# A gated linear attention and a maxout FFN in one kernel: the 64x64 products of two units put into one run

## The chip, the cores and the metric

One core of one Trainium2 chip runs the whole program. The metric is the device time of one execution in microseconds, as the median of the runs shown. The engines are named as in the profile: PE (TensorE matmul, with its weight loads as PEld), DVE (VectorE), ACT (ScalarE), POOL (GpSimd) and SP, whose queue issues nearly all of the DMAs.

## The reference

The first half is a linear attention with a gate for each feature, for 4 batches, 8 heads, 768 tokens and 48 features; its output goes, token by token, into an FFN whose hidden layer is the largest of three products. All is float32.

```python
f = 1.0 / (1.0 + np.exp(-f_logit))
for t in range(S):
    state = f[:, :, t, :, None] * state + np.einsum('bhd,bhe->bhde', k[:, :, t], v[:, :, t])
    y[:, :, t] = np.einsum('bhd,bhde->bhe', q[:, :, t], state)
x = attn_out.transpose(0, 2, 1, 3).reshape(B * S, H * D)          # 3072 x 384
h = np.maximum(np.maximum(x @ w1, x @ w2), x @ w3)                # 384 -> 768
out = h @ w_out                                                   # 768 -> 384
```

## The kernel before

**Units.** The attention is cut into 24 units. A unit is a chunk of 64 tokens (`C`) of two batches (`a` = 0, 1) with all 8 heads (four pairs `hp`, each with an even and an odd head, `par` = 0, 1). Unit u works on chunk u // 2 and on batches 2(u % 2) and 2(u % 2) + 1, so unit u continues the states that unit u - 2 left. Four units make a group of 512 tokens (`GRP`, `TOK`), and each group has one FFN.

**The products of a unit on PE.** They are 64x64 products, four to a set (one for each `par` and `a`), which run beside each other in the four quarters of the array:

- `pairs` (L400): keys times queries of the chunk, into the two-bank tile `a`; DVE then multiplies them by the causal mask into `at` (L403);
- `sums` (L437): keys times values, the chunk's contribution to the state, into the other half of the same banks; DVE adds it to the decayed state (`new_state`, L452), and POOL decays the result for the unit after next (`carry`, L361);
- `values` (L419): `at` times values, into the two-bank tile `y`; ACT then reads one element of `y` into `seen` (L426);
- the products of the queries with the state, in `finish` (L508), added to the same `y`; then ACT copies `y` into the FFN's input `xT` (L515), and `pack` moves rows of it by DMA.

Before that, DVE turns the loaded blocks (L300), runs two scans (L333, L351), and turns the scaled keys back, 16 transposes a unit in four parts (`keys_by_blocks`, L386); POOL makes the scaled keys `kh` (L344) and queries `qh` (L355).

**The FFN on PE.** Full 128x128 products: `inputs_by_pairs` (L884) and `outputs_by_pairs` (L633), for groups 1 to 5; group 0 has its own form with L546 and L787. Both use four PSUM banks, two called `p` and two called `tr`. In the inputs, three pairs of hidden blocks n = 0, 1, 2 go through seven steps; the steps of n use one `tr` bank `B[n]` and one `p` bank `A[n]`. `third(n)` ends with DVE reading `B[n]` (L927), `fourth(n)` with DVE reading `A[n]` (L934) and taking the maximum with the rest (L935). In the outputs, `a` is a `p` bank and `b` and `c` are the two `tr` banks; `add(o_of(0, 0), b, 0)` has DVE read `b` (L641).

**What sets the order.** The order is written by hand: inside `tc.manual_schedule()` each engine has its instructions in the order of the code, and semaphores are added where one reads or overwrites what another has written. The FFN is a generator that yields the cost of what it just issued; `fill(ns)` lets it go on until the costs come to ns. The main loop over units calls `fill` five times a unit, and the attention's steps lie between these calls. In unit u the 64x64 products come in one piece: `values(u - 1)`, `sums(u - 1)`, `pairs(u)`, `finish(u - 1)`. After the last unit, `values(23)` and `finish(23)` come as two more pieces. The name "run of unit u" below means that piece.

**PSUM.** Eight banks: `p` 2, `tr` 2, `a` 2, `y` 2. The pools hand out `p` and `tr` banks in turn.

## Time and profile before

| what | value |
|---|---|
| runs | 405.4, 407.33, 407.48 us; median 407.33 us |
| profiled execution, span from first to last instruction | 403.7 us |
| median of the runs less that span | 3.6 us |
| PE busy | 390.9 us (97%) |
| DVE busy | 297.7 us (74%) |
| POOL busy | 256.4 us (64%) |
| ACT busy | 180.9 us (45%) |
| mean granted TensorE clock | 0.999 |

The execution that was profiled has a span of 403.7 us; its own time with what lies around the span is not given apart, so a change in the span is added to the median of the runs. In rows of the timeline the columns are start in us from the span's start, duration in us, engine, line, operation, out<-in, and the number of instructions merged into the row; a float32 product is two instructions, so that the 16 products of a step stand as x32. A duration reaches to the modelled end of the last matmul, which lies past the start of what follows.

### The profile page before, as it was taken

What the parts mean: (1) busy time and instruction counts of PE and PEld (TensorE: products, weight loads), DVE (VectorE), ACT (ScalarE), POOL (GpSimd) and SP (SyncE); (2) the same over time, 40 slices, a digit from 0 to 9 for tenths busy, and PEclk for the clock granted to TensorE, in tenths of its full rate; (3) what the DMA queues carried; (4) which work ended last, traced back from release to release, by engine and by line L of the source; (5) the groups of instructions that cost most, each with busy time, mean ns of one, the idle gap of its engine ahead of it and who ended that gap; (6) DMA issues with size and microseconds to landing.
All of it is one profiled execution on the core that took longest, in us unless ns stands there. A gap on an engine that the chain in (4) does not pass through costs nothing.

```text
span 403.7 us, 11683 instructions
## 1 busy us (share of the span) xinstructions
PE 390.9 (97%) x4658; PEld 339.7 (84%) x4658; DVE 297.7 (74%) x572; ACT 180.9 (45%) x431; POOL 256.4 (64%) x283
## 2 busy tenths in 40 slices
PE   5988999999999999999999999999999999999995
PEld 4766765559998889998889988899988889988995
DVE  6997897999989999897998997998995450002600
ACT  3478787422224442345532344523354425586120
POOL 2189695879997697296587277667477850435700
PEclk9999999999999999999999999999999999999999
DMA  8999986767574576576635477634573003541002
GB/s 171 233 282 284 279 214 89 153 92 150 82 96 114 69 154 135 104 120 84 131 104 97 62 113 88 156 78 81 75 157 91 1 19 87 143 136 70 2 19 63
DMA packets 181611, 47.21 MB, mean 117 GB/s; under 512 B 160497, under 2 KB 179249, under 8 KB 181553
## 3 DMA queue, kind: packets, MB, share of 16 engines
q1 hardware_dynamic: 177536, 45.52, 54.7%
q10 hardware_dynamic: 4016, 0.91, 1.1%
q8 instruction: 37, 0.61, 0.6%
q14 instruction: 22, 0.17, 0.1%
HBM read 37.75 MB, written 4.72 MB: 105 GB/s over the span
## 4 chain that ended last, share of the span: by engine, by line
PE 90%; SPq 4%; DMA 1%; ACT 1%; issue 1%; POOL 1%; DVE 0%
PE p L884 20%; PE p L633 18%; PE tr L884 16%; PE tr L633 14%; PE p L546 7%; PE y L419 3%; PE p L787 3%; PE a L400 2%; PE y L508 2%; PE a L437 2%; SPq L178 2%; DMA v_ld<-in_v_dram 1%; SPq L164 1%; SPq L222 1%; PE tr L295 1%
## 5 line engine op out<-in xcount | busy, mean ns | idle before, releaser
L386 DVE STREAM_TRANSPOSE ks<-kh 32x128 f32<-32x128 f32 x256 | 77.5, 303 | 11.5 <-POOL kh L344 7.4
L884 PE MATMUL tr<-xT,placed 128*128 128x256 f32 x180 | 44.4, 384 | 0.0
L343 POOL COPY ends<-r 128x8 f32<-128x8 f32 x24 | 8.6, 358 | 48.1 <-DVE r L333 48.1
L884 PEld LDWEIGHTS tr<-xT,placed 128*128 128x128 f32 x180 | 33.5, 190 | 4.9
L344 POOL TENSOR_TENSOR kh<-kt,r 128x512 f32<-128x512 f32 x18 | 31.9, 1772 | 8.5 <-DVE kt L300 8.5
L333 DVE TENSOR_TENSOR_SCAN r<-gate,from_one 128x520 f32<-128x520 f32 x24 | 33.2, 1382 | 5.4 <-ACT gate L312 2.8
L546 PE MATMUL p<-xT,w_in 128*128 128x256 f32 (+1 forms) x108 | 33.9, 458 | 3.0 <-POOL w_in L756 1.9
L597 POOL TENSOR_TENSOR w_in<-hm 128x256 f32<-128x256 f32 x18 | 13.3, 737 | 32.2 <-DVE hm L935 29.4
L515 ACT COPY xT<-y 64x256 f32<-64x256 f32 (+1 forms) x60 | 22.1, 368 | 22.4 <-PE y L508 21.7
L351 DVE TENSOR_TENSOR_SCAN prod<-gate,from_inv 128x520 f32<-128x520 f32 x24 | 31.6, 1317 | 0.0
L884 PE MATMUL tr<-xT,w_in 128*128 128x256 f32 x120 | 30.8, 379 | 0.0
L641 DVE TENSOR_TENSOR o<-tr,w_in 128x384 f32<-128x384 f32 (+1 forms) x11 | 5.7, 521 | 33.4 <-PE tr L633 29.0
L884 PE MATMUL p<-w_in,placed 128*128 128x256 f32 x120 | 30.4, 382 | 0.0
L633 PE MATMUL p<-placed,hm 128*128 128x192 f32 x144 | 29.7, 333 | 0.0
L546 PEld LDWEIGHTS p<-xT,w_in 128*128 128x128 f32 x108 | 19.5, 190 | 12.0 <-issue 6.0
L884 PE MATMUL p<-xT,placed 128*128 128x256 f32 x120 | 29.2, 379 | 0.0
L633 PE MATMUL tr<-w_out,w_in 128*128 128x192 f32 x144 | 28.6, 326 | 0.0
L927 DVE TENSOR_TENSOR hm<-tr,hm 128x512 f32<-128x512 f32 x15 | 10.3, 684 | 22.8 <-PE tr L884 15.9
L262 POOL TENSOR_TENSOR w_in<-top_bits,rest_bits 128x384 uint32<-128x384 uint32 x18 | 21.7, 1216 | 7.2 <-DVE top_bits L256 4.3
L884 PEld LDWEIGHTS p<-w_in,placed 128*128 128x128 f32 x120 | 22.4, 190 | 4.4 <-issue 1.5
L638 ACT COPY w_in<-p 128x384 f32<-128x384 f32 x15 | 7.2, 479 | 41.0 <-PE p L633 41.0
L284 ACT ACTIVATE raw<-top_bits 128x384 f32<-128x384 f32 x48 | 25.2, 526 | 0.4
(168 smaller groups left out, 995.6 us busy)
## 6 DMA issues: line engine op xcount, KB each, us to landing
raw<-in_moe_w_dram SPq DMA_DIRECT2D x24, 384.0 KB, 4.4
v_ld<-in_v_dram SPq DMA_DIRECT2D x48, 96.0 KB, 3.4
placed<-in_moe_w_dram SPq DMA_DIRECT2D x12, 384.0 KB, 6.3
out_dram<-o SPq DMA_DIRECT2D x45, 96.0 KB, 2.2
placed<-in_moe_w_out_dram SPq DMA_DIRECT2D x6, 384.0 KB, 5.4
f_ld<-in_f_logit_dram SPq DMA_DIRECT2D x36, 64.0 KB, 2.7
k_ld<-in_k_dram SPq DMA_DIRECT2D x36, 64.0 KB, 2.5
q_ld<-in_q_dram SPq DMA_DIRECT2D x36, 64.0 KB, 2.6
```

What stands on the lines that cost most here:

```text
L262: nc.gpsimd.tensor_tensor(dst, by(top), by(rest), op=ALU.add)
L284: nc.scalar.activation(over, size, AF.Relu, scale=(-1 / HI_MIN, 1.0)[step - 1], bias=(1.0, -HI_END * (1 - 2.0 ** -24))[step - 1], accum_ou ...
L333: nc.vector.tensor_tensor_scan(r[:, 0:LEN][:, ::-1], flat(gate)[:, ::-1], flat(from_one)[:, ::-1], 1.0, op0=ALU.mult, op1=ALU.max)
L344: (nc.vector if u < BY_ROWS else nc.gpsimd).tensor_tensor(kh.rearrange("p h a t -> p a h t"), kt, by_batch(r[:, 1:LEN + 1].rearrange("p (x ...
L351: nc.vector.tensor_tensor_scan(flat(prod), flat(gate_tiles[u % 2]), flat(from_inv[u % 2]), 1.0, op0=ALU.mult, op1=ALU.max)
L386: nc.vector.transpose(ks[n * 32:(n + 1) * 32, :, par, e0:e0 + 32], kh[p0:p0 + 32, :, a, t0:t0 + 32])
L419: nc.tensor.matmul(y[o:o + DP, a, hp * C:(hp + 1) * C], lhsT=v_ld[s, 2 * hp + par, :], rhs=d["at"][s, par, hp, :], start=(hp == 0), stop=F ...
L515: nc.scalar.copy(xT[o, :, t0 + a * C:t0 + (a + 1) * C], y[i, a, 0:HP * C].rearrange("p (h t) -> p h t", h=HP))
L546: nc.tensor.matmul(p if w < TOK else p.rearrange("p (two t) -> p two t", two=2), lhsT=w_in[i][:, kt, j * 128:(j + 1) * 128], rhs=x[:, t.st ...
L597: engine.tensor_tensor(dst, x, y, op=op)
L633: nc.tensor.matmul(b[:, p * HD:(p + 1) * HD], lhsT=x, rhs=w, start=id(b) not in begun, stop=True, skip_group_check=True)
L884: nc.tensor.matmul(b[:, j * HALF:(j + 1) * HALF], lhsT=w[:, (2 * n + j) * 128:(2 * n + j + 1) * 128], rhs=x, start=begin and j == 0, stop= ...
```

## The change

From unit 9 on, a run has the 64x64 products of two units. Units 9, 11, ..., 23 have no such products of their own. The runs of units 10, 12, ..., 22 and a last one, called unit 24, hold in this order: `pairs(u - 1)`; `sums` of u - 2 and half of u - 1 (`sums_apart`); `values(u - 2)`; `values(u - 1)`; the other half of the sums; DVE's two additions `new_states`; `pairs(u)`; the state products of u - 2 and of u - 1 (`with_state`); then the copies `to_x` of both and one `pack`. The run of unit 24 has neither sums nor `pairs(u)`.

The two units share the tiles: `y` and the pairs take the left or the right half of each of their banks. The sums go to one `p` and one `tr` bank of the FFN, those that it would use next; `fill_to_free` lets the FFN go on to a place where these hold nothing that is still needed (after a `fourth`, or after `add(o_of(0, 0), b, 0)` in the outputs). The `p` and `tr` banks become fixed tiles in turn, and the states of both units one tile each. The parts of `keys_by_blocks` move to other places between the calls of `fill`, of which there are still five a unit.

```diff
+            def psum(nm, ahead=False):
+
+                t = rooms[nm][turn_of[nm] % 2]
+                turn_of[nm] += not ahead
+                return t
...
+            all_states = keep.tile([128, 2, 2, HP * D], FP32, name="st")
+            states = [all_states[:, :, bp] for bp in range(2)]
+            all_carried = keep.tile([128, 2, 2, HP * D], FP32, name="state")
...
 def pairs(u, p=None):
+                at0 = u % 2 * HP * C if u > FIRST else 0
...
-                        nc.tensor.matmul(p[t, par, hp * C:(hp + 1) * C], lhsT=kh[r, hp, a, :], rhs=qh[r, a, hp, :],
+                        nc.tensor.matmul(p[t, par, at0 + hp * C:at0 + (hp + 1) * C], lhsT=kh[r, hp, a, :], rhs=qh[r, a, hp, :],
...
-            def values(u):
+            def values(u, y=None, first=True):
...
+                if u >= FIRST:
+                    y = y[:, :, u % 2 * HP * C:(u % 2 + 1) * HP * C]
...
+            def sums_apart(u, lanes, hps=range(HP)):
+
+                d, v_ld = ready[u], v_tiles[u % NLD]
+                Y = u % 2 * HP * D
+                for hp in hps:
+                    for par, a in FOUR:
+                        s = slice(a * C, (a + 1) * C)
+                        nc.tensor.matmul(lanes[a][par * DP:(par + 1) * DP, Y + hp * D:Y + (hp + 1) * D],
+                                         lhsT=d["ks"][s, 2 * hp + par, :], rhs=v_ld[s, 2 * hp + par, 0:D],
+                                         start=True, stop=True)
+
+            def new_states(lanes):
+                for a in range(2):
+                    flat_of = lambda t: t[:, a].rearrange("p b x -> p (b x)")
+                    nc.vector.tensor_tensor(flat_of(all_states), lanes[a][:, 0:2 * HP * D], flat_of(all_carried), op=ALU.add)
...
+            def fill_to_free():
+                while not free[0]:
+                    advance()
...
-                for u in range(GRP, NU):
+                for u in range(GRP, NU + 1):
...
+                    run = u <= FIRST or u % 2 == 0
...
+                    elif run:
+                        fill_to_free()
+                        room_of_unit, y = room_of_pairs(), room_of_y()
+                        lanes = [psum(nm, ahead=True) for nm in ("p", "tr")]
+                        pairs(u - 1, room_of_unit)
+                        if u < NU:
+                            sums_apart(u - 2, lanes)
+                            sums_apart(u - 1, lanes, range(HP // 2))
+                        values(u - 2, y)
+                        values(u - 1, y, False)
+                        if u < NU:
+                            sums_apart(u - 1, lanes, range(HP // 2, HP))
+                            new_states(lanes)
+                            pairs(u, room_of_unit)
+                        for i in (2, 1):
+                            with_state(u - i)
+                        for i in (2, 1):
+                            to_x(u - i, xT)
...
+                    if u > FIRST:
+                        keys_by_blocks(u, 0)
+                        if not run:
+                            keys_by_blocks(u, 1)
+                        fill(part)
...
+                    elif run:
+                        carry(u)
+                        carry(n)
+                        keys_by_blocks(u, 1)
+                        keys_by_blocks(u, 2)
                     else:
-                        values(u)
+                        keys_by_blocks(u, 2)
+                        keys_by_blocks(u, 3)
...
-                    if n == NU:
-                        finish(u, xT)
-                        pack(3, 3, xT, both)
-                        packed[u // GRP] = xT
-                    keys_by_blocks(n, 0)
-                    fill(part - 1000 if u < 2 * GRP else part)
-                    keys_by_blocks(n, 1)
+                    if u < FIRST:
+                        keys_by_blocks(n, 0)
+                        fill(part - 1000)
+                        keys_by_blocks(n, 1)
+                    elif u == FIRST:
+                        fill(part)
+                    elif run:
+                        keys_by_blocks(u, 3)
```

**What it does to the order.** The lines of the changed kernel are later by some: `pairs` is L416, `sums_apart` L529, `values` L441, the state products L551, the FFN's inputs L930 and outputs L676; on DVE `at` is L419, `new_states` L536, the readers of the FFN's banks L973, L980, L981 and L684, the transposes of the keys L401. The words in square brackets name the semaphores that an instruction waits for, by the engine that raises them.

PE at the run of unit 14, before (`fourth(0)` of the inputs ends, then values and sums of unit 13, pairs of 14, state products of 13, and the inputs go on):

```order
L884 MATMUL p_2364<-w_in1_64,placed1_135 128x256
L419 MATMUL y_2574<-at_2427,v_ld1_127 64x64 [waits DMAHW4_49,DVE_49,PE_49]
L419 MATMUL y_2574<-at_2427,v_ld1_127 64x64
L419 MATMUL y_2574<-at_2427,v_ld1_127 64x64 [waits DMAHW5_49]
L419 MATMUL y_2574<-at_2427,v_ld1_127 64x64 x13
L437 MATMUL a_2573<-v_ld1_127,ks_2337 64x48 [waits DVE_49]
L437 MATMUL a_2573<-v_ld1_127,ks_2337 64x48
L437 MATMUL a_2573<-v_ld1_127,ks_2337 64x48 [waits DVE_49] x2
L437 MATMUL a_2573<-v_ld1_127,ks_2337 64x48 x12
L400 MATMUL a_2573<-qh_2509,kh_2502 64x64 [waits Pool_49]
L400 MATMUL a_2573<-qh_2509,kh_2502 64x64 x15
L508 MATMUL y_2574<-qh_2296,state_2313 48x64 [waits Activation_49]
```

The same engine and place after the change, the start of the run: the last product of `fourth(0)` into bank `p1_89`, the pairs of unit 13, and the first sums of unit 12, which go to that same `p1_89` and to `tr0_86`:

```order
L930 MATMUL p1_89<-w_in1_64,placed1_139 128x256
L416 MATMUL a_2397<-qh_2207,kh_2200 64x64 [waits PE_49]
L416 MATMUL a_2397<-qh_2207,kh_2200 64x64 x15
L529 MATMUL p1_89<-v_ld0_130,ks_2176 64x48 [waits DMAHW1_49,DVE_49]
L529 MATMUL p1_89<-v_ld0_130,ks_2176 64x48
L529 MATMUL tr0_86<-v_ld0_130,ks_2176 64x48 [waits DMAHW2_49]
```

And the middle of that run: values of unit 12, values of unit 13 in the other half of the same tile `y_2398`, and the rest of the sums. The value that the Activation semaphore has to reach there is the one that the copy `seen` of unit 12 raises, the DVE value is that of `at` of unit 13, and the DVE value in the fence above is that of L980, which reads `p1_89`:

```order
L441 MATMUL y_2398<-at_2132,v_ld0_130 64x64 [waits PE_49]
L441 MATMUL y_2398<-at_2132,v_ld0_130 64x64 x15
L441 MATMUL y_2398<-at_2415,v_ld1_131 64x64 [waits DVE_49,Activation_49]
L441 MATMUL y_2398<-at_2415,v_ld1_131 64x64 x15
L529 MATMUL p1_89<-v_ld1_131,ks_2303 64x48 x2
```

What moved: the run has 256 products instead of 128 and starts with pairs; its values wait for a mask product and for a copy of the same run, and its sums for the reader of an FFN bank.

DVE before and at the run of unit 16, before (turning and scanning for unit 16, sums of the FFN's input, keys, the reader of the outputs' bank `b`, keys, then `at` of unit 16):

```order
L300 STREAM_TRANSPOSE kt<-k_ld_116 128x512
L351 SCALAR_TENSOR_TENSOR prod<-gate_99,from_inv_95 128x520
L300 STREAM_TRANSPOSE qt<-q_ld_118 128x512
L597 TENSOR_TENSOR xT_146<-xT_146 128x2x128
L597 TENSOR_TENSOR s_last<-xT_146 128x256
L386 STREAM_TRANSPOSE ks<-kh 32x4x32 x4
L641 TENSOR_TENSOR o<-tr,w_in_63 128x2x192
L386 STREAM_TRANSPOSE ks<-kh 32x4x32 x8
L403 TENSOR_TENSOR at<-a,mask 128x512
L452 TENSOR_TENSOR st_142<-a,state 128x384
```

The same place after the change (`at` of unit 15, the two state sums and `at` of unit 16 belong to the run):

```order
L310 STREAM_TRANSPOSE kt<-k_ld_120 128x512
L364 SCALAR_TENSOR_TENSOR prod<-gate_103,from_inv_99 128x520
L310 STREAM_TRANSPOSE qt<-q_ld_122 128x512
L640 TENSOR_TENSOR xT_150<-xT_150 128x2x128
L640 TENSOR_TENSOR s_last<-xT_150 128x256
L401 STREAM_TRANSPOSE ks<-kh 32x4x32 x8
L684 TENSOR_TENSOR o<-tr_87,w_in_63 128x2x192
L419 TENSOR_TENSOR at<-a,mask 128x512
L536 TENSOR_TENSOR st<-p_89,state 128x384
L536 TENSOR_TENSOR st<-tr_87,state 128x384
```

What moved: eight transposes of the keys (of unit 15, whose `kh` is a unit old) stand ahead of the reader of `b` instead of four of unit 16; and the bank `tr_87` that this reader frees is the one that the run's sums are written to.

## The prediction

> **What bounds the kernel now.** I read the page first: busy shares, slices and the chain.

> ```profile
> span 403.7 us, 11683 instructions
> PE 390.9 (97%) x4658; PEld 339.7 (84%) x4658; DVE 297.7 (74%) x572; ACT 180.9 (45%) x431; POOL 256.4 (64%) x283
> PE   5988999999999999999999999999999999999995
> DVE  6997897999989999897998997998995450002600
> PEclk9999999999999999999999999999999999999999
> PE 90%; SPq 4%; DMA 1%; ACT 1%; issue 1%; POOL 1%; DVE 0%
> ```

> PE is full from the fourth slice to the last, at full clock, and it is 90% of the chain that ended last. So a microsecond saved in PE's own sequence is a microsecond of the span, and so is each one in which PE is made to wait. DVE is second, at nine tenths for as long as there is attention (to slice 30). A window there says how near it is:

> ```profile
> 200.00:220.00 20.00, 20.00 (x227) 18.68 (x227) 18.54 (x36) 7.04 (x18) 15.34 (x16) 1.00 0.52 113
> ```

> DVE, the fourth figure, works 18.5 of 20 us. Whatever makes PE wait for DVE will find it late more often than idle.

> **What the change removes: nine changes between full and 64x64 products.** The timeline of PE around the run of unit 14:

> ```profile
> 188.34 1.03 PE L884 MATMUL p<-xT,w_in 128*128 128x256 f32 x4
> 189.20 1.03 PE L884 MATMUL p<-rest_bits,placed 128*128 128x256 f32 x4
> 190.07 1.03 PE L884 MATMUL p<-w_in,placed 128*128 128x256 f32 x4
> 191.02 0.69 PE L419 MATMUL y<-at,v_ld 64*64 64x64 f32 x32
> 191.54 0.63 PE L437 MATMUL a<-v_ld,ks 64*64 64x48 f32 x32
> 191.99 0.66 PE L400 MATMUL a<-qh,kh 48*64 48x64 f32 x32
> 192.47 0.63 PE L508 MATMUL y<-qh,state 48*48 48x64 f32 x32
> 193.03 1.99 PE L884 MATMUL tr<-xT,placed 128*128 128x256 f32 x8
> 194.86 0.38 PE L884 MATMUL p<-w_in,placed 128*128 128x256 f32 x1
> ```

> Four full products take 0.865 us from start to start (188.34, 189.20, 190.07), but the four ahead of the run take 0.95: 0.09 lost going in. The run lasts 2.01 us where four steps of 0.465 (between L437's 0.45 and L400's 0.48) would be 1.86: 0.16 at its two ends. The eight after it take 1.83 instead of 1.73: 0.10 more. Together 0.36 us a run, the same to 0.01 at the other whole runs.

> ```profile
> 117.77 0.69 PE L419 MATMUL y<-at,v_ld 64*64 64x64 f32 x32
> 329.26 0.69 PE L419 MATMUL y<-at,v_ld 64*64 64x64 f32 x32
> 332.68 0.67 PE L508 MATMUL y<-qh,state 48*48 48x64 f32 x32
> ```

> From unit 9 (the first row) on there are 15 runs before and the two pieces of unit 23 (the other rows), 17; after, eight: units 10, 12, ..., 24. The numbers of products and of FFN steps are the same. **Gain: 9 x 0.36 = 3.24 us.**

> **What it adds, first: the copy `seen` inside the run.** Before, it is raised and used 0.93 us apart, with sums and pairs between (191.54 to 192.47). After, PE goes from the values of u - 2 straight to those of u - 1, whose first product waits for the copy made after the last product of u - 2, as the order shows. That round trip is in the trace:

> ```profile
> 191.79 0.15 ACT L426 COPY seen<-y 1x1 f32<-1x1 f32 x1 [0.77 <-PE y L419]
> 66.78 0.14 ACT L426 COPY seen<-y 1x1 f32<-1x1 f32 x1
> 66.97 0.67 PE L508 MATMUL y<-qh,state 48*48 48x64 f32 x32
> ```

> In unit 14 ACT had been idle for it and the copy ended at 191.94; at 66.92 a copy ended late and PE's L508 started 0.05 after. So PE could go on at 191.99, where its next step began at 191.54: 0.45 us. L508 at 66.97 also took 0.67 rather than 0.63: 0.04 to get going again. **Loss: 0.45 in each of units 10 to 22, 7 x 0.45 = 3.15.** Bounds: 0.3 (the copy and one hand-over) to 0.8 (ACT busy with a 0.48 us copy).

> [...]

> **Second: sums in the bank that `fourth` has just filled.** In units 10, 14, 18 and 22 the free place is the end of a `fourth`, and the sums' `p` bank is the one that DVE's L934 must still read.

> ```profile
> 191.20 0.69 DVE L934 SCALAR_TENSOR_TENSOR hm<-hm,p 128x512 f32<-128x512 f32 x1 [1.48 <-PE p L884]
> 191.81 0.68 DVE L935 SCALAR_TENSOR_TENSOR hm<-hm,top_bits 128x512 f32<-128x512 f32 x1
> L403 DVE TENSOR_TENSOR at<-a,mask x24: 678/692/693, 12.1 to 324.4; 128x512 f32<-128x512 f32 x24
> ```

> This is that very `fourth(0)`, with DVE waiting for it: the read ends at 191.89, PE hears of it at 191.95. The run's pairs, 0.51 with the start, would let the sums begin at 191.53. **Loss: 4 x 0.42 = 1.68**, with 0 as the lower bound and 1.5 each where DVE is late. The mask product `at` of u - 1 then runs from 192.42 to 193.11 (0.69 behind L935), and the values that need it come at 191.95 + 0.70 of sums + 0.46 + 0.45 = 193.56: hidden, by 0.4 us. If DVE is later than that, PE waits for it too. DVE itself stands idle from there until the last sums, about 1.4 us a run.

> **Third: sums in the outputs' bank `b`.** In units 12, 16 and 20 the `tr` bank of the sums is `b`, which PE left 5 us ago but which DVE reads (L641, now L684) only when it gets there. Before, at unit 16:

> ```profile
> 206.67 0.69 DVE L927 TENSOR_TENSOR hm<-tr,hm 128x512 f32<-128x512 f32 x1
> 207.37 1.26 DVE L386 STREAM_TRANSPOSE ks<-kh 32x128 f32<-32x128 f32 x4
> 208.64 0.69 DVE L403 TENSOR_TENSOR at<-a,mask 128x512 f32<-128x512 f32 x1
> 209.81 1.26 DVE L386 STREAM_TRANSPOSE ks<-kh 32x128 f32<-32x128 f32 x4
> 220.37 1.24 DVE L386 STREAM_TRANSPOSE ks<-kh 32x128 f32<-32x128 f32 x4 [1.08 <-POOL kh L344]
> 221.65 0.56 DVE L641 TENSOR_TENSOR o<-tr,w_in 128x384 f32<-128x384 f32 x1
> 205.22 1.03 PE L884 MATMUL tr<-xT,placed 128*128 128x256 f32 x4
> 208.18 1.13 PE L884 MATMUL p<-rest_bits,placed 128*128 128x256 f32 x4
> 221.16 0.69 PE L419 MATMUL y<-at,v_ld 64*64 64x64 f32 x32
> ```

> DVE reads `b` from 221.65 to 222.21, after the run has begun. From `third(2)`'s reader at 206.67 to there are 15.54 us. After the change `at` and its state sum (208.64 to 209.81) are not in this stretch, the wait for `kh` goes, since the keys are of the unit before, and four transposes more (1.27) come in: 15.54 - 1.17 - 1.08 + 1.27 = 14.56. It cannot begin before `third(2)` ends, which after the change is right ahead of `fourth(2)` (208.18, call it F): the four products reach 0.17 past F, DVE starts 0.10 later (191.20 against 190.07 + 1.03). So `b` is free at F + 0.27 + 14.56 + 0.05 = F + 14.88. PE from F to the run takes 221.16 - 208.18 = 12.98, less 0.11 for no run ahead, and 0.51 of pairs: the sums want the bank at F + 13.38. **Loss: 3 x 1.5 = 4.50.** Bounds: 0, if DVE has less to do there, and 2.6, since a row of the same view shows what its operations can take beside POOL:

> ```profile
> 203.62 1.75 DVE L935 SCALAR_TENSOR_TENSOR hm<-hm,top_bits 128x512 f32<-128x512 f32 x1
> ```

> That is 1.06 above its 0.68. I take 1.5, as the rows of this very stretch give it; the 1.75 falls in a place where DVE would otherwise wait for `third(2)`.

> **Unit 24** has no sums to hide behind. `at` of 23 ends 0.74 + 0.69 + 0.06 = 1.49 us after the pairs begin, values of 22 are over at 0.97: 0.52 us; then the state products wait for the last `seen`: 0.45. **Loss 0.97.** Sixteen restarts in all (7 + 4 + 3 + 2) at 0.04: **0.64**.

> **What costs nothing.** Moved keys, scans and `carry` keep their number; the keys' `kh` and the decayed state are now made a unit ahead, and DVE no longer waits for POOL there. `pack` comes as often as before; after unit 24's run some 38 output products of 0.325 us, 12.4 us, hide copies of 2.3, the transfer and POOL's sums of `xT`. The state sums end, by DVE, at about the time that PE leaves the run; if later, the next `tr` step waits for the rest.

> **Sum.** -3.24 + 3.15 + 1.68 + 4.50 + 0.97 + 0.64 = +7.7 us on the span of 403.7. On the median of 407.33, which is 3.6 above the span, that is 415.0.

> **Rivals.**
> - *The run's waits are covered (faster).* Had PE work between, as at `seen` before, only the switches would count: 407.33 - 3.24 = 404.1. The point is 0.40 us of waiting a run, on average over the eight. For it: PE never waits for `seen` from unit 9 on now. Against: the round trip alone measures 0.45, with nothing put between.
> - *DVE reaches `b` in time*, the rest as forecast: 415.0 - 4.5 - 0.12 = 410.4. For it: DVE loses its waits for `kh` and reads `b` only 0.5 us after the run's start now. Against: the 14.56 against 13.1 us above.
> - *Neither bank makes PE wait*: 410.4 - 1.68 - 0.16 = 408.6, which one can hardly tell from no change.
> - *DVE becomes the bound.* With 18.5 of 20 us busy and 1.4 us more of standing still in each run, one slow operation (+1.06) in each half of a group is handed to PE: 415.0 + 7 x 1.06 = 422.4.

> **How the numbers follow.** Forecast 0.55, with a range of its own from 412 to 418; `b` in time 0.15; neither bank 0.10; faster 0.10; DVE the bound 0.10. The likeliest gives 415.0. From 408 to 420 leaves out the faster case and most of the last. A measurement of this kernel tells about 0.5% (2 us) from no change: faster 0.10, same 0.10 (the case of 408.6), slower 0.80.

> **What would show it.** Right: PE idle within the runs, before the second values (released by ACT's `seen`) in every one, before the first sums in units 10, 14, 18, 22 (by L980) and longer in 12, 16, 20 (by L684); eight pieces of 64x64 products from unit 9 on; PE's busy time down by about 3 us. Wrong: no idle time there, or idle time of PE outside the runs, at the FFN's own banks; or a wait for `at` longer than for `seen`, which would mean that DVE is further behind than I have it.

## The result and the profile after

The changed kernel takes 432.64 us (median of 6 runs, 429.97 to 436.66) against 406.67 before (6 runs, 405.4 to 409.13): 1.062 times as long, with an interval from 1.057 to 1.067; this ratio leaves out the run of 436.66, which was in the chip's slower state. Forecast were 415.0, with 420 as the upper end. The sign was right, the size was a third of what came: 7.7 us forecast, 26 measured, both on the medians and on the two profiled spans (403.7 and 429.7).

First the head of the page of after, and the row of the granted clock:

```profile
span 429.7 us, 11709 instructions
PE 399.2 (93%) x4658; PEld 348.8 (81%) x4658; DVE 298.0 (69%) x572; ACT 181.2 (42%) x431; POOL 252.0 (59%) x283
PEclk9999999999999997999999999999799999999999
```

PE now stands still for 7% of the span, and the clock row, all nines before, has a 7 in two slices. What PE stood still for is in its waits (line, releaser: us in total, times, longest); the rows not shown here are those of the first 60 us and small ones:

```profile
PE tr L529 <- DVE o L684: 9.3, 3, 4.0
...
PE y L551 <- issue: 3.4, 3, 1.6
PE y L441 <- ACT seen L448: 2.3, 8, 0.4
...
PE p L529 <- DVE hm L980: 1.0, 4, 0.3
PE tr L930 <- issue: 0.6, 1, 0.6
```

Three of the five are the forecast's: the sums wait for `b` (L684) in 3 runs and for L980 in 4, the second values wait for `seen`. The two rows with "issue", waits that the list puts down to no releaser, are new. So is the clock. By microsecond around the run of unit 12 (PE busy with its instructions, granted clock, DMA share, GB/s):

```profile
162.00:163.00 1.00, 0.77 (x37) 1.00 0.30 54
166.00:167.00 1.00, 0.18 (x8) 0.65 0.00 0
168.00:169.00 1.00, 1.00 (x44) 0.50 0.00 0
172.00:173.00 1.00, 1.00 (x48) 0.50 0.00 0
173.00:174.00 1.00, 1.00 (x28) 0.94 0.00 0
```

From 166.29 to 173.12 PE had half its clock; this began in the last half microsecond of the longest wait (162.77 to 166.81). The same follows the waits in units 16 (3.4 us from 234.56) and 20 (6.8 us from 299.42): 17.1 us in all. What that costs is seen in the state products: the same 64 instructions take 2.08 us in unit 16, at half clock, and 1.07 in unit 10, at full clock. So I put the loss at half of the 17.1, 8.5 us, an estimate.

```profile
135.05 1.07 PE L551 MATMUL y<-qh,state 48*48 48x64 f32 x64
236.07 2.08 PE L551 MATMUL y<-qh,state 48*48 48x64 f32 x64
```

With PE's starts taken from the trace, the 26.0 us come together like this (in us; a wait costs its idle time and about 0.18 more, since idle time counts only from the modelled end of the product before: in unit 10, 0.26 idle were 0.44 from start to start):

```
                                             forecast   measured
changes of shape spared, 9 runs                -3.2       -1.8
second values wait for seen, 7 runs            +3.2       +3.1
sums wait for L980, 4 runs                     +1.7       +1.7
sums wait for b (L684), 3 runs                 +4.5       +9.8
unit 24                                        +1.0       +1.1
restarts (now in the rows above)               +0.6
waits for "issue", 4                            -         +4.5
half clock behind the waits for b               -         +8.5
sum                                            +7.7      +26.9 of 26.0
```

### The profile page after: what moved, and what is told of

Read it like the earlier page. It is cut to its first block, busy times and chain, and to the rows that moved or that the text cites. A ratio compares the mean times of both kernels' runs of the same rounds, so it can differ in the third digit from the quotient of the medians.

```text
span 429.7 us, 11709 instructions
## 1 busy us (share of the span) xinstructions
PE 399.2 (93%) x4658; PEld 348.8 (81%) x4658; DVE 298.0 (69%) x572; ACT 181.2 (42%) x431; POOL 252.0 (59%) x283
## 4 chain that ended last, share of the span: by engine, by line
PE 75%; DVE 12%; issue 3%; POOL 3%; SPq 2%; ACT 2%; DMA 1%; DVEq 0%; ACTq 0%; POOLq 0%
PE p L930 15%; PE tr L930 14%; PE p L676 14%; PE tr L676 9%; PE p L589 6%; PE y L441 3%; PE p L833 3%; PE y L551 3%; DVE ks L401 3%; PE a L416 2%; DVE r L346 1%; PE p L529 1%; DVE prod L364 1%; POOL w_in L272 1%; SPq L607 1%
## 5 line engine op out<-in xcount | busy, mean ns | idle before, releaser
L401 DVE STREAM_TRANSPOSE ks<-kh 32x128 f32<-32x128 f32 x256 | 77.3, 302 | 4.2 <-POOL kh L357 0.4
L930 PE MATMUL tr<-xT,placed 128*128 128x256 f32 x180 | 43.6, 382 | 0.6 <-issue 0.6
L745 POOL TENSOR_TENSOR o<-top_bits,w_in 128x384 f32<-128x384 f32 x5 | 5.2, 1036 | 66.1 <-ACT w_in L681 53.0
L930 PEld LDWEIGHTS tr<-xT,placed 128*128 128x128 f32 x180 | 33.8, 190 | 5.7 <-issue 1.0
L966 POOL TENSOR_TENSOR top_bits<-top_bits,top 128x512 f32<-128x512 f32 x15 | 19.9, 1324 | 26.3 <-ACT top_bits L965 26.3
L684 DVE TENSOR_TENSOR o<-tr,w_in 128x384 f32<-128x384 f32 (+1 forms) x11 | 5.7, 522 | 41.8 <-PE tr L676 39.2
L364 DVE TENSOR_TENSOR_SCAN prod<-gate,from_inv 128x520 f32<-128x520 f32 x24 | 32.8, 1366 | 0.0
L930 PE MATMUL tr<-xT,w_in 128*128 128x256 f32 x120 | 30.8, 379 | 0.0
L676 PE MATMUL p<-placed,hm 128*128 128x192 f32 x144 | 30.5, 339 | 0.0
L357 POOL TENSOR_TENSOR kh<-kt,r 128x512 f32<-128x512 f32 x18 | 27.2, 1509 | 5.5 <-DVE kt L310 5.5
L930 PE MATMUL p<-w_in,placed 128*128 128x256 f32 x120 | 30.4, 382 | 0.0
L930 PE MATMUL p<-xT,placed 128*128 128x256 f32 x120 | 29.2, 379 | 0.0
L973 DVE TENSOR_TENSOR hm<-tr,hm 128x512 f32<-128x512 f32 x15 | 10.4, 692 | 26.9 <-PE tr L930 19.9
L676 PE MATMUL tr<-w_out,w_in 128*128 128x192 f32 x144 | 28.7, 327 | 0.0
L640 POOL TENSOR_TENSOR w_in<-hm 128x256 f32<-128x256 f32 x18 | 13.3, 738 | 24.7 <-DVE hm L981 24.7
L930 PEld LDWEIGHTS p<-w_in,placed 128*128 128x128 f32 x120 | 22.4, 190 | 4.2 <-issue 1.1
```

The source lines that it names most:

```text
L357: (nc.vector if u < BY_ROWS else nc.gpsimd).tensor_tensor(kh.rearrange("p h a t -> p a h t"), kt, by_batch(r[:, 1:LEN + 1].rearrange("p (x ...
L364: nc.vector.tensor_tensor_scan(flat(prod), flat(gate_tiles[u % 2]), flat(from_inv[u % 2]), 1.0, op0=ALU.mult, op1=ALU.max)
L401: nc.vector.transpose(ks[n * 32:(n + 1) * 32, :, par, e0:e0 + 32], kh[p0:p0 + 32, :, a, t0:t0 + 32])
L640: engine.tensor_tensor(dst, x, y, op=op)
L676: nc.tensor.matmul(b[:, p * HD:(p + 1) * HD], lhsT=x, rhs=w, start=id(b) not in begun, stop=True, skip_group_check=True)
L930: nc.tensor.matmul(b[:, j * HALF:(j + 1) * HALF], lhsT=w[:, (2 * n + j) * 128:(2 * n + j + 1) * 128], rhs=x, start=begin and j == 0, stop= ...
```

## Experiments

**Two theories for what the forecast lacked.** *Clock*: the half clock behind the waits for `b` comes from PE's standing still in them (4.05, 2.63 and 2.62 us), and it costs half of the 17.1 us that it lasts. *Block edges*: PE's instructions come in blocks of 256, and where small products use one up in some 2 us, the next is not there yet. For the second speak the places of the "issue" waits. I numbered all of PE's instructions by their starts, the 4658 products, the 4658 weight loads and the 91 others: the last ones before the four waits have the numbers 1985, 5057, 6593 and 8129, which are all 193 plus a multiple of 256. The page agrees, in its list of queues: 37 x 256 = 9472, and PE has 9407 instructions in the trace.

```profile
q8 instruction: 37, 0.61, 0.6%
```

The rivals: the clock falls without cost; the "issue" waits belong to the state products (L551), at which they stand. In the timeline of unit 18, this is how one looks, after 61 of the 64 instructions of the state products:

```profile
266.02 1.07 PE L551 MATMUL y<-qh,state 48*48 48x64 f32 x61
268.71 0.31 PE L551 MATMUL y<-qh,state 48*48 48x64 f32 x3 [1.63 <-issue]
```

### Work for PE in the wait for b

```
 pairs(u - 1, room_of_unit)
+if u < NU and u % GRP == 0:
+    for _ in range(6):
+        nc.tensor.matmul(lanes[0].rearrange("p (n t) -> p n t", n=4), lhsT=ident,
+                         rhs=ident.unsqueeze(1).to_broadcast([128, 4, 128]), start=True, stop=True)
```

> Six products of ident with 512 columns (0.43 us each, 2.6 us together, results overwritten) are put into the free p lane behind the first pairs of the runs in units 12, 16 and 20, where PE otherwise stands still for 4.05, 2.63 and 2.62 us until L684 has read b. Nothing is released earlier. Theory (the half clock of 6.8, 3.4 and 6.8 us behind these three waits is caused by PE standing still): the granted clock stays at 1.00 throughout, the waits of L529 for L684 shrink to about 1.4, 0 and 0, and half of 17.1 us is saved: 8.5 us, 432.6 - 8.5 = 424 us. Rival (the clock falls for another reason, such as the many small products in a row, or the fall costs nothing because DVE is late anyway): the clock still falls and the time stays at 432 to 434 us.

Measured: 437.68 us (1.077, 1.074 to 1.080), slower than after. The six products took 5.35 us a time, not 2.6: each is two products of the trace. So 16.1 us of work stand where 9.3 of waiting were (+6.8). The half clock shrank from 17.1 to 3.4 us (-6.8), and the waits at the edges grew:

```profile
PE y L551 <- issue: 8.2, 7, 1.7
```

+4.2 us and the restarts: the sum is about the 5.0 measured. With the size of the filling right, three products:

> The kernel of after with three products of 512 columns in the waits for L684 of units 12, 16 and 20 (each is two of the trace, 0.89 us, so three are 2.7 us; six were 5.35 and reached past the waits). Nothing is released earlier, so the waits as such stay: about 1.4 us of standing still in unit 12, none in 16 and 20, and PE at work instead. Theory (half clock from standing still, at half of 17.1 us): 8.5 us less, against 0.5 to 1.7 more at the block edge of each of these runs, now at full speed (3.2 together): 432.6 - 5.3 = about 427. If the clock holds and the time does not fall at all, the half clock was not what cost the time.

Measured: 429.19 us (1.058, 1.054 to 1.063), 3.45 less than after on the medians (the two intervals overlap; the profiled spans are 1.9 apart). Nothing was released earlier and PE had 8.0 us of useless products; the wait for `b` is down to 1.1 us in unit 12, the half clock to 3.4 us, and the waits at the edges are up to 7.5:

```profile
PE y L551 <- issue: 7.5, 6, 2.0
PE tr L529 <- DVE o L684: 1.1, 1, 1.1
```

-6.8 by the clock, +3.5 at the edges: -3.3. It is these two terms, more than the medians, that show what the half clock costs. Half of the gain was handed on to the block edges: 1.8 in units 16 and 20, which at half clock had not stopped there, 1.3 in unit 14 and 0.5 in unit 6.

### The keys behind the reader of b

```
-    else:
+    elif u % GRP != 3:
         keys_by_blocks(u, 2)
         keys_by_blocks(u, 3)
...
 pairs(u - 1, room_of_unit)
+if u % GRP == 0:
+    keys_by_blocks(u - 1, 2)
+    keys_by_blocks(u - 1, 3)
```

> In the units ahead of the outputs' runs (11, 15, 19) the last two blocks of key transposes (8 transposes, 2.53 us of DVE) are issued behind the run's first pairs, so that DVE's L684 and at come ahead of them. Theory (b is late because of these 2.53 us on DVE): PE's wait for L684 falls from 4.05, 2.63 and 2.62 us to about 1.7, 0.4 and 0.5, and PE waits up to 0.95 us in its stead for the last keys ahead of the second part of the sums: -6.7 + 2.9 = -3.9 us. If about 1.8 us of standing still, in pieces, no longer brings the half clock, 8.5 us more go: 420 us; if it still does, 429 us. Rival (the place of the keys does not matter, L684 waits for something else): 432 to 434.

Measured: 432.12 us (1.065, 1.057 to 1.072), no change. L684 came earlier, but the first part of the sums needs these very keys, and PE waited for them instead:

```profile
PE tr L529 <- DVE ks L401: 6.7, 6, 2.0
...
PE tr L529 <- DVE o L684: 1.4, 1, 1.4
```

8.1 for 9.3 us, and the clock fell as before. I had put only the second part of the sums behind these keys; a miss. In either order PE waits there for DVE's work.

### The run later

```
 fill_to_free()
+for _ in range(4 if u < NU and u % GRP == 0 else 0):
+    advance()
```

> The outputs' runs (units 12, 16, 20) come four FFN steps later (2.6 us of products that use only bank a, with as much less FFN work behind), so that DVE has read b when the sums want it. Theory (the wait for L684 and the half clock behind it cost 9.3 + 0.6 and 8.5 us): PE's wait for L684 falls to about 1.5 in unit 12 and 0 in 16 and 20, the clock stays at 1.00, and the three runs now meet the block edges at full speed, 0.5 to 1.7 us each (3.5 together): 432.6 - 8.4 - 8.5 + 3.5 = about 419. Rival 1 (the half clock costs nothing by itself): 428. Rival 2 (DVE falls back further, since PE is earlier at every stage, and the wait comes back): 428 to 433.

Measured: 423.11 us (1.043, 1.040 to 1.047): 9.5 less than after, by nothing but four FFN steps in another place. In the profiled execution, one of 420.54 us, the waits for L684 are gone, and the clock is 1.00 through the runs of all units. That leaves

```profile
PE y L551 <- issue: 6.4, 6, 1.7
...
PE p L529 <- DVE hm L980: 2.0, 4, 1.2
PE p L676 <- ACT w_in L681: 1.7, 3, 0.6
```

The median is four us above the 419 expected. The profile shows three things that were not in that sum: the steps that were moved ahead wait for ACT's copy of bank `a` (1.7), L980 came later once (+1.0), and a transfer of `v` was late by 1.1 in one of the first units, where nothing was changed. The other three executions, 422.6 to 424.4 us, had a mean clock of 0.996; no profile shows where in them it fell.

### The order within the run

First the values of u - 2 ahead of the sums:

```
 pairs(u - 1, room_of_unit)
+values(u - 2, y)
 if u < NU:
     sums_apart(u - 2, lanes)
     sums_apart(u - 1, lanes, range(HP // 2))
-values(u - 2, y)
 values(u - 1, y, False)
```

> In each run the values of u - 2 stand right behind the first pairs, ahead of the state sums; the sums then lie between the two values. Theory (waits inside the run are simply uncovered): the wait for seen (0.44 with the restart, in 7 runs) and that for L980 (0.435, in 4 runs) go, that for L684 becomes 0.3 shorter in 3: -3.1 - 1.7 - 0.9 = -5.7, 427 us. Second theory (the code of a block of 256 instructions of PE is fetched while the block before is used, about 3.3 us, and a run uses one up in 2.0 us): what is won in units 14, 18 and 22 comes back as a longer wait at the block's edge there (up to 0.9 each): about 429 to 430 us, with PE's waits for nothing that the profile shows growing from 0.62, 1.63, 1.01 to up to 1.5, 2.5, 1.9. Rival (the order within the run is of no account): 432 to 434.

Measured: 430.66 us (1.060, 1.053 to 1.068). The waits for `seen` in the runs and for L980 are gone, that for L684 is 7.9, `at` takes 1.5, and the edges went from 3.4 and 0.6 to

```profile
PE y L551 <- issue: 4.6, 4, 1.6
PE y L441 <- DVE at L419: 1.5, 4, 0.4
```

and the clock was halved for 20.5 us instead of 17.1. Of 5.7 us that were won by the order, 2.0 arrived on the medians, less than the runs scatter (427.97 to 433.31). Together with the later runs, and with all sums ahead of the second values:

> As the kernel with the outputs' runs four steps later, and in every run the order first pairs, values of u - 2, all state sums, values of u - 1, last pairs, state products. The waits for seen and L980 are then covered (-3.1 - 1.7), at of u - 1 is waited for about 0.35 in 4 runs (+1.4), and the denser runs lose more at the block edges (up to 0.9 in each of 6): from about 419 to 416 without and 420 with that last term. If the sum of all waits but the block edges' goes and the time still stays at 416 or more, the edges are what holds a merged run above before.

Measured: 418.58 us (1.034, 1.027 to 1.041), the best of the merged kernels; the profiled span is 415.6, 11.9 above before. In that execution the clock is 1.00 throughout, there is no wait for `b`, and `seen` is waited for only in unit 24 (0.7 with its last). What remains is mostly the edges:

```profile
PE y L551 <- issue: 7.3, 6, 1.5
...
PE p L676 <- ACT w_in L681: 1.7, 3, 0.6
PE p L529 <- DVE hm L980: 0.7, 1, 0.7
PE tr L930 <- issue: 0.6, 1, 0.6
```

### The edges by themselves

The kernel of before, with longer runs and nothing else:

```
-for hp in range(HP):
+for hp in [hp for _ in range(5 if u > 2 * GRP and u % 2 == 0 else 1) for hp in range(HP)]:
     for par, a in FOUR:
         ...
         nc.tensor.matmul(p[t, par, hp * C:(hp + 1) * C], lhsT=kh[r, hp, a, :], rhs=qh[r, a, hp, :],
```

> The kernel of before; only the pairs of units 10, 12, ... 22 are computed five times over into the same place, 128 small products more in a row (256 instructions with their weight loads), so that these 7 runs have 512 instructions, as the merged runs have; no bank, copy or DVE work is changed. By the products alone: 7 x 128 x 0.015 = 13.4 us, 406.2 + 13.4 = 419.6. Theory (the next block of 256 instructions is there some 3.3 us after PE has begun one, and small products use one up in 2.0): PE stops in or right behind most of these runs at a block's edge, 1.3 to 1.8 us each, 7 x 1.5 = 10.5 us more: about 430. Rival (the waits in the merged runs come from their banks or their state products): no such waits, 419 to 421.

Measured: 429.51 us (2 runs, 426.87 and 432.15; the profile is of the first), where the products alone give 419.6. Two banks of sums, half banks and merged units are not in this kernel, yet it has the same waits, in or right behind six of the seven long runs and behind none of the short ones:

```profile
PE y L508 <- issue: 4.9, 4, 1.5
...
PE tr L884 <- issue: 1.1, 1, 1.1
PE p L633 <- issue: 0.9, 1, 0.9
```

The clock stayed at 0.999. This is the test that the rival, "it is the state products or the banks", does not survive: in L633 and L884 FFN products wait.

Then the edges were shifted against the program of after, with 64 and then 32 small products in the wait for `b` of unit 12:

```
 pairs(u - 1, room_of_unit)
+if u == 3 * GRP:
+    for i4 in range(64):
+        r, o = 0, i4 % 2 * 64
+        nc.tensor.matmul(lanes[0][o:o + 64, 0:64], lhsT=ident[r:r + 64, 0:64],
+                         rhs=ident[r:r + 64, 0:64], start=True, stop=True)
```

> 64 small products (64x64, results overwritten) stand in the wait for b of unit 12, 128 instructions of PE with their weight loads; they end within that wait of 4.05 us, so that nothing else moves. Theory (PE stops at the edges of its blocks of 256 instructions): all edges behind it come 128 instructions earlier in the program. PE's unexplained waits of 1.63 and 1.01 us leave the state products (L551) of units 18 and 22 and stand about 128 instructions earlier in these runs, in the second values, sums or pairs, and that of 0.62 us in unit 14, now in the FFN product behind the run, moves into the run; each about 0.8 to 1.6 us. Rival (the state products wait for something of their own, the decayed state or a transfer): the waits stay on L551 with the same lengths.

Measured (one run): 432.88 us, and the waits stayed on L551 in units 18 and 22 (1.70 and 1.23). That speaks for neither, since 64 products in the code are 128 of the trace, with their weight loads 256 instructions: one whole block. With half:

> As the kernel with 64 small products in the wait of unit 12, but with 32: each is two products of the trace, so 64 were a whole block of 256 instructions and moved no edge against the runs; 32 are half a block. Theory (block edges): the waits of units 18 and 22 leave L551 and stand some 360 to 380 instructions into the run, in its second pairs (L416); that behind the run of unit 14 moves to the first state products (L551), near the 394th. Rival (the state products wait for something of their own): they stay on L551 of 18 and 22 where they are, at the end of these products.

Measured (one run): 436.26 us. The waits of units 18 (1.28) and 22 (0.73) left the state products for the second pairs, and that behind the run of unit 14 moved into it, onto L551 (1.12):

```profile
PE y L551 <- issue: 2.1, 2, 1.1
PE a L416 <- issue: 2.0, 2, 1.3
```

All places, by PE's instruction number; each is 193 + 256 k:

```
after            1985   5057   6593   8129                       k = 7, 19, 25, 31
six products     1985   4289   5057   5825   6593   7361   8129  k = 7, 16, 19, 22, 25, 28, 31
before, longer   4801   5825   6849   7873   8897   9921         k = 18, 22, 26, 30, 34, 38
half a block     1985   5057   6593   8129                       now on L551, L551, L416, L416
```

The packets of queue 8, which the page calls "instruction", go with these waits. The list of queues has 37 of them, of 16 KB each, for 9407 instructions of PE, and 44 for the 11200 of the kernel with longer runs. In the trace of after, PE enters a block at 264.99, has used it up at 266.87 and goes on at 268.71; in between lies one packet on that queue, from 266.46 to 267.33. So it is with every wait of over half a microsecond at an edge, in all these kernels: PE goes on 1.2 to 1.6 us after the packet has ended (in after 1.25, 1.41, 1.38 and 1.49, in units 6, 14, 18 and 22). From unit 10 on, 2.9 to 4.7 us pass from entering the block to going on, where PE used it up in 1.8 to 3.0 (in after 3.89, 3.72 and 3.12, where it was used up in 2.89, 1.88 and 1.89). The 3.3 us from entering a block to the next that two expectations take were an estimate of mine.

Could they be kept out of the runs? Once by work between the two halves of the run, in the kernel with the later, reordered runs:

```
     sums_apart(u - 1, lanes)
-values(u - 1, y, False)
 if u < NU:
     new_states(lanes)
+for _ in range(3 if u < NU and u % GRP == 0 else 0):
+    advance()
+values(u - 1, y, False)
+if u < NU:
     pairs(u, room_of_unit)
```

> As the kernel with the later, reordered runs, but in units 12, 16 and 20 three FFN steps (1.46 us of products, no bank of the run) stand between the state sums and the values of u - 1, so that the run's 512 instructions of PE become two stretches of 256. Theory (block edges): the waits of 1.32, 1.06 and 1.23 us in these three runs go, with 0.3 of restart each: -4.5; three more changes of shape cost 3 x 0.2 to 0.36: +0.8; 418.6 - 3.7 = 415. The waits in units 18 and 22 stay. Rival (the waits come with the merged run whatever its length): 419 to 420.

Measured: 422.37 us (1.042, 1.037 to 1.047), 3.8 more than without the split. The waits in the three runs are gone, as the theory says: none of their stretches of 256 has one. But PE stops behind them for DVE, three times, and longer at the edges of units 18 and 22 (2.15 and 1.43); behind the first of these the clock was halved for 3.4 us (mean clock 0.996):

```profile
PE y L551 <- issue: 4.6, 3, 2.2
...
PE tr L930 <- DVE o L684: 4.2, 3, 1.4
```

So the three waits went as expected, and the gain did not come. L684 here is the reader of the outputs' last `tr` bank, which the next group's inputs need. DVE is late there because of the split: in unit 12 it stands for 2.25 us until the second pairs have come behind the three steps, its `at` begins at 170.82 instead of 169.00, and this L684 at 179.80 instead of 178.21.

And once by shifting all edges, with 44 small products in front of everything:

```
+lead = psum("p", ahead=True)
+for i4 in range(44):
+    nc.tensor.matmul(lead[i4 % 2 * 64:i4 % 2 * 64 + 64, 0:64], lhsT=ident[0:64, 0:64],
+                     rhs=ident[0:64, 0:64], start=True, stop=True)
 sigmoids(0)
```

> As the kernel with the later, reordered runs, with 44 more small products (176 instructions of PE) in the first microseconds, while PE waits for its first transfer. All block edges come 176 instructions earlier in the program, 0.69 of a block. With 3.8 us from the moment that PE's sequencer, some 64 instructions ahead, enters a block until the next one is there, the waits at the edges from unit 10 on fall from 5.4 to about 3.5 us by my replay of the trace: 418.6 - 2 = 416 to 417, and no wait stands at the places of the kernel without the shift. Rival (the waits belong to the state products): nothing changes, 418 to 419.

Measured: 419.95 us (1.036, 1.032 to 1.040), no gain. The places moved, to the second values and pairs, with none left on L551:

```profile
PE a L416 <- issue: 3.9, 3, 1.4
PE y L441 <- issue: 2.3, 3, 1.5
```

but 6.2 us remain where my replay had 3.5. Its 3.8 us lie between the 3.89, 3.72 and 3.12 of after; that PE's sequencer is some 64 instructions ahead was an assumption of mine that no run shows, and why the replay fell short is not shown either. Behind the wait of unit 10 the clock was halved as well, for 3.4 us from 137.96 (mean clock 0.996), which is 1.7 lost. A merged run of 512 instructions holds two edges wherever they lie.

No kernel here beats the one before.

## Why the prediction was right or wrong

- *The waits inside the run, by place and releaser*: right, all four kinds. In unit 24 the list puts the first wait down to `seen`, but `at`, which the forecast named, ended later (at 360.40; PE went on at 360.50). One sign of being right failed: PE's busy time was to fall by about 3 us and rose from 390.9 to 399.2; in the best merged kernel, at full clock, it is 390.8. Unit 10 shows two of the waits:

```profile
131.20 0.69 PE L416 MATMUL a<-qh,kh 48*64 48x64 f32 x32
132.15 0.26 PE L529 MATMUL p<-v_ld,ks 64*64 64x48 f32 x2 [0.26 <-DVE hm L980]
...
132.88 0.66 PE L441 MATMUL y<-at,v_ld 64*64 64x64 f32 x32
133.84 0.69 PE L441 MATMUL y<-at,v_ld 64*64 64x64 f32 x32 [0.29 <-ACT seen L448]
```

  From start to start the pairs took 0.95 instead of 0.51 and the values 0.96 instead of 0.52: 0.44 each, forecast 0.42 and 0.45. Half a bank did not free PE from the other unit's copy, as the order said: the second values wrote other columns and waited (0.29 idle in unit 10). They did so because the order has the wait; no run here lets the two go on at once, so whether they could is not shown.
- *The term of `b`* was mis-sized: 3 x 1.5 forecast, 9.8 measured. PE's side was right: in unit 16 the sums began 13.39 us after `fourth(2)`, where the forecast had 13.38. DVE's side failed. From the reader of `third(2)` at 216.51 to the end of L684 it took 15.97 us instead of 14.56, since the scan and the last two sums, which I carried over at their durations before, together took longer, with POOL at work beside them:

```profile
222.79 1.72 DVE L346 TENSOR_TENSOR_SCAN r<-gate,from_one 128x520 f32<-128x520 f32 x1
...
227.28 0.74 DVE L640 TENSOR_TENSOR xT<-xT 128x256 f32<-128x256 f32 x1
227.94 1.41 DVE L640 TENSOR_TENSOR s_last<-xT 128x256 f32<-128x256 f32 x1
229.37 2.53 DVE L401 STREAM_TRANSPOSE ks<-kh 32x128 f32<-32x128 f32 x8
231.92 0.56 DVE L684 TENSOR_TENSOR o<-tr,w_in 128x384 f32<-128x384 f32 x1
```

  Before, the same scan took 1.24 and the two sums 0.96 and 0.41:

```profile
211.85 1.24 DVE L333 TENSOR_TENSOR_SCAN r<-gate,from_one 128x520 f32<-128x520 f32 x1
...
218.00 0.96 DVE L597 TENSOR_TENSOR xT<-xT 128x256 f32<-128x256 f32 x1
218.88 0.41 DVE L597 TENSOR_TENSOR s_last<-xT 128x256 f32<-128x256 f32 x1
```

  +0.48 and, from the first start to the last end of the two sums, +0.78: 1.26 of the 1.41. In the later trace POOL is in the middle of an operation when the scan starts (L640, from 222.69 for 0.73) and runs L368 from 227.70 to 229.07 beside the second sum; before, it was idle during that scan. The upper bound that I worked out from just such a row, 2.6, is nearly what units 16 and 20 lost (2.63 and 2.62 idle, 2.8 with the 0.18); I took the lower value because the rows "of this very stretch" gave it. Unit 12 (4.05) lay outside the bound: there DVE also waited 0.95 for POOL and 0.55 for a transfer on the way.
- *The half clock* had no term at all. The trace of before, whose PE is busy for 97%, has a clock of 1.00 from 10.20 to 402.73 and gave no price for it. The forecast put PE to rest for about 2 us in each of three runs (1.5 and 0.45), and for 3 at its bound, and priced only the rest. The clock cost 8.5 us, half of the 17.1.
- *The block edges* had no term either: the sum took a run of 512 instructions for two of 256. Before, no run was longer than 256 instructions. The edges cost 4.5 us, and more as the other waits went (7.9 idle in the best merged kernel).
- *The spared changes of shape* were over-sized: inside the merged run nothing is spared (3.98 us without its waits, twice 2.00 before). What is spared is the slower FFN product ahead of and behind a run (0.31 and 0.32 instead of 0.22), 0.2 per run, not 0.36. So the rival "the waits are covered" could not have reached 404.1, but 405.5.
- *DVE the bound, 422.4*: wrong as told. DVE is busy for 69% and waits itself; it holds PE up for longer than forecast only at `b`, in three places.

One wait at an edge, 0.73 us, stands in unit 6, where the code is that of before, which has none there. The packet of that block came late: it began 3.5 us after PE had entered the block (79.20 against 75.70), and before, 0.8 us after. Why it came late stays open.

## What to carry to other kernels

Before moving small products together, count PE's instructions in the longest stretch without a large product: here up to 256 cost nothing but for one wait in unit 6, and 512 cost 0.2 to 2.2 us in most runs at full clock, nearly always more than the 0.2 that merging spares. A wait of PE that is to be accepted should be priced twice, for itself and for the clock behind it (here 9.3 us, and 8.5 of the 17.1 at half clock), and even useless work of the right length in it was no loss here (429.19 us against 432.64). And where a wait hangs on how far a busy engine lags, take its operations at their longest durations in the profile, not at those of the place they come from.

## What the runs showed of the hardware

**Block edges show behind small products, not behind large ones.** In after, the four waits lie at places 193 + 256 k of PE's instructions. Of large products, 128, with their weight loads 256 instructions, last over 20 us at 0.16 to 0.22 from start to start; where PE used such a stretch up from 204.27 to 228.37, it did not stand still at the end. 128 small ones last 2.0, and in unit 18 PE waited 1.63 more.
